# Spectral filter and expert layer: spectral steps of two bins by 256 columns, with the first-factor transform turned over and its output sent through DRAM

## The chip, the cores and the metric

The kernel runs on one core of one Trainium2 chip. The metric is the device time of one execution in microseconds (us). A timed run is made without the profiler; the profile is one more execution, with its own time. TensorE is called PE below, VectorE DVE, ScalarE ACT, GpSimd POOL and SyncE SP, as in the rows of the profile.

## The reference

The input x has 8 sequences of 2496 rows and 256 columns. Along the rows each sequence is filtered in the frequency domain, and each filtered row then goes through one of eight experts.

```python
X = np.fft.rfft(x, axis=1)                      # x: (8, 2496, 256)
Y = X * (filt_r + 1j * filt_i)[None]
y = np.fft.irfft(Y, n=2496, axis=1)             # -> 19968 rows of 256
logits = y @ w_gate                             # 8 experts
expert_idx = argmax(logits); gate = softmax(logits)[expert_idx]
out[row] = gate * (relu(y[row] @ w1[e]) @ w2[e])   # w1: 256x1024, w2: 1024x256
```

## The kernel before

The transform of length 2496 = 39 x 64 is done in two factors, as float32 matrix products. The work is cut into 16 units u: a sequence b and a half h of 128 columns, u = 2b + h.

- `loadx` brings x of one unit into tiles `x` of 39-row groups, three groups on 117 partitions. `forward1` (L263) does the 39-point factor: a piece of x is the stationary operand and the constant `a1` the moving one, so the result stands with the 128 columns on partitions. ACT (and DVE for one of six pieces) copies it, in strides, into the tile `T` (L271).
- A step t is one fifth of a unit: four frequency bins. `spec1` turns `T` back with four TensorE transposes (L311) and ACT copies the result to `z` (L317). `spec2` does the 64-point factor (L326, PSUM tile `px`): four products of 128x128 by 128 columns. `filt_` multiplies by the filter on DVE (L345 to L347), `join` adds the two parts on POOL (L355), `spec3` does the 64-point factor of the inverse (L366, PSUM `pi`), and ACT copies it to `U` (L371). There are 80 steps.
- When a sequence is in `U`, `route1` to `route6` compute the gate and each row's place (L497 and after, PSUM `plw`, `pgl`, `pl`, `pp`), `inv1` turns `U` (L633, PSUM `pg`), `inv2` does the 39-point factor of the inverse (L647, PSUM `py`), and `inv3` scatters the rows, sorted by expert, to the DRAM tile `xs` by indirect DMAs of POOL (L158).
- Beside this, the weights of the experts are loaded (`wf`), brought to a common scale (`w_max` on DVE, L399; `w_hi` on ACT, L465; `w_lo` on DVE, L470), cut into two float16 parts `wh` and stored to DRAM (`wscr`).
- The expert stage reads 161 blocks of 128 sorted rows (`xb`), transposes them by DMA (`xt`), and does the two layers on TensorE (L1038, PSUM `ph`; L1064, PSUM `po`).

The order of the instructions on every engine is written out by hand. Each piece of work is put in a list with a key in steps, `at(key, f, ...)`, the list is sorted by key, and each engine gets its instructions in that order. An engine takes its queue strictly in order; a DMA is issued by the engine in whose queue it stands, and a DMA whose buffer isn't free blocks what stands behind it on that queue. The keys that matter here:

```python
K = {"s2": 1.394, "sr": 1.65, "si": 1.85, "s3": 3.6, "f": 0.063, "fd": 0.75, "w": 6.0, "wp": 4.1}
RT = (0.0, 0.4, 0.45, 0.9, 1.3, 1.7, 2.2, 2.5, 2.9, 3.3)
```

`K["s2"]` is where `spec2` of a step stands behind the step's own key, `K["s3"]` where `spec3` does, and `RT` are the offsets of the ten routing pieces behind the end of a sequence. The PSUM pools are `pF` with 4 banks (for `f`, `pt`, `px`, `pi`, `pg`), `pD` with one, `pY` with two (for `py`) and `pW` with one.

## Time and profile before

| | |
|---|---|
| timed runs | 1387.08, 1389.56, 1389.87 us, median 1389.56 |
| the profiled execution | 1385.97 us, its span 1384.1 us |
| first spectral work, to the first `plw` (sequence 0 done) | 0 to 79.58 us |
| six sequences, from the `plw` of sequence 0 to that of sequence 6 | 79.58 to 428.27 us |
| the rest of the spectral stage, to the first `ph` | 428.27 to 476.54 us |
| the expert stage | 476.54 to 1384.08 us |

`plw` is the first routing product of a sequence and stands right behind its last `spec3`, so the time between two of them is the time of a sequence. Groups in the profile give the busy time, the mean of one instruction and the idle time of the engine ahead of it. Instructions of ACT and PE overlap their neighbours at both ends, so the time that one costs in a full queue is the distance between two starts, shorter than its mean. In the chain of waits the rows are already cut to what each added to the time.

### The profile page before, as it was taken

To read this page: it belongs to the slowest core of one execution; us is meant where nothing else is said; L and a number is where in the kernel's file an instruction comes from. 1 tells how busy PE (TensorE), PEld (TensorE's weight loads), DVE (VectorE), ACT (ScalarE), POOL (GpSimd) and SP (SyncE) were. 2 spreads that over 40 slices of the span, in tenths; PEclk is the share of its full clock that TensorE was granted. 3 is DMA by queue.
4 is the path that set the end of the run, shared out by engine and by line. 5 is a ranking of instruction groups with operands and counts; after the bars stand their busy time and mean duration, and the time that the engine had idled before them with its cause. 6 is when DMAs were issued, how large, how long until landed. Compare 5 with 4: busy or idle time off the path is not lost.

```text
span 1384.1 us, 39837 instructions
## 1 busy us (share of the span) xinstructions
PE 1311.9 (95%) x14855; PEld 1176.2 (85%) x14855; DVE 834.0 (60%) x2391; ACT 853.8 (62%) x1444; POOL 465.2 (34%) x446
## 2 busy tenths in 40 slices
PE   6889999998999799999999989999999999999997
PEld 5778777777777688899999988998999998998997
DVE  1688879888797564455555544555555554555552
ACT  3567667766676546566666655665665665666664
POOL 3627485574745615422111111111111111111111
PEclk9899999999999999999999999999999999999999
DMA  9746565564644533793463396337337336336431
GB/s 181 206 141 201 167 197 178 165 182 149 200 132 126 157 90 94 203 299 91 115 156 82 97 321 205 77 78 190 77 78 193 79 75 191 79 75 162 111 73 43
DMA packets 198278, 197.76 MB, mean 143 GB/s; under 512 B 104008, under 2 KB 177339, under 8 KB 189827
## 3 DMA queue, kind: packets, MB, share of 16 engines
q1 hardware_dynamic: 178142, 151.96, 40.5%
q0 software_dynamic: 19472, 42.51, 10.7%
q8 instruction: 118, 1.93, 0.6%
q10 hardware_dynamic: 468, 0.72, 0.2%
q14 instruction: 78, 0.63, 0.2%
HBM read 344.12 MB, written 61.56 MB: 293 GB/s over the span
## 4 chain that ended last, share of the span: by engine, by line
PE 54%; DMA 7%; DVE 3%; issue 3%; SPq 2%; ACT 1%; POOL 1%; POOLq 0%; DVEq 0%; ACTq 0%
PE ph L1038 26%; PE po L1064 24%; DMA wa<-wscr 3%; DMA wb<-wscr 2%; PE py L647 1%; DMA xt<-xs 1%; SPq L943 1%; SPq L1025 1%; PE pg L633 1%; DMA xs<-yt,dest 1%; PE px L326 1%; PE pi L366 1%; DVE hl L1052 1%; POOL out_dram L158 0%; ACT xs L1017 0%
## 5 line engine op out<-in xcount | busy, mean ns | idle before, releaser
L1038 PE MATMUL ph<-xt,wa 128*128 128x128 f16 x7728 | 462.2, 220 | 12.3 <-DMA wa<-wscr 9.6
L1038 PEld LDWEIGHTS <-wa 128*128 128x128 f16 x7728 | 447.6, 98 | 24.5 <-DMA wa<-wscr 12.7
L1064 PE MATMUL po<-wb,hh 128*128 128x256 f16 x2576 | 431.1, 273 | 4.7 <-ACT ot L1080 2.6
L1052 DVE TENSOR_TENSOR hl<-hs,hh 128x512 f16<-128x512 f32 x322 | 222.8, 692 | 352.6 <-ACT hh L1046 263.8
L158 POOL DMA_INDIRECT out_dram<-ot,t x161 | 157.9, 981 | 672.7 <-DVE xs L1018 571.5
L1064 PE MATMUL po<-wb,hl 128*128 128x256 f16 x1288 | 351.1, 273 | 0.0
L1064 PEld LDWEIGHTS <-hh 128*128 128x128 f16 x2576 | 245.4, 98 | 34.5 <-issue 6.0
L1044 ACT ACTIVATE hs<-ph 128x512 f32<-128x512 f32 x322 | 192.2, 597 | 85.5 <-PE ph L1038 68.4
L158 POOL DMA_INDIRECT xs<-yt,dest x176 | 185.6, 1055 | 120.4 <-issue 62.7
L1017 ACT ACTIVATE xs<-xb,s 128x256 f16<-128x256 f32 x161 | 81.8, 508 | 223.1 <-DVE s L1007 218.4
L1046 ACT CAST hh<-hs 128x512 f16<-128x512 f32 x322 | 198.9, 618 | 10.1
L1064 PEld LDWEIGHTS <-hl 128*128 128x128 f16 x1288 | 126.1, 98 | 14.7
L355 POOL TENSOR_TENSOR p<-tr,ti 128x512 f32<-128x512 f32 x71 | 91.1, 1283 | 93.3 <-DVE ti L347 77.2
L371 ACT COPY U<-pi 128x512 f32<-128x512 f32 (+1 forms) x80 | 87.4, 1092 | 53.5 <-PE pi L366 53.5
L1018 DVE SCALAR_TENSOR_TENSOR xs<-xb,s,xs 128x256 f16<-128x256 f32 x161 | 78.0, 484 | 51.0 <-ACT xs L1017 51.0
L326 PEld LDWEIGHTS px<-z,bm 128*128 128x128 f32 x640 | 80.3, 194 | 20.3 <-issue 10.6
L366 PE MATMUL pi<-cm,p 128*128 128x128 f32 (+1 forms) x640 | 87.7, 281 | 6.2 <-POOL p L355 5.9
L326 PE MATMUL px<-z,bm 128*128 128x128 f32 x640 | 87.9, 281 | 5.6 <-ACT z L317 4.4
L647 PE MATMUL py<-gh,dm 117*117 117x512 f32 x176 | 91.9, 603 | 1.4 <-ACT gh L639 1.4
L263 PE MATMUL f<-a,x 117*128 117x117 f32 (+1 forms) x628 | 87.7, 278 | 5.4 <-ACT U L371 2.1
L366 PEld LDWEIGHTS pi<-cm,p 128*128 128x128 f32 x640 | 80.0, 196 | 9.5 <-POOL p L355 6.3
L263 PEld LDWEIGHTS f<-a,x 117*128 117x128 f32 (+1 forms) x628 | 78.5, 192 | 10.4 <-ACT U L371 3.0
(171 smaller groups left out, 1315.5 us busy)
## 6 DMA issues: line engine op xcount, KB each, us to landing
wb<-wscr SPq DMA_DIRECT2D x133, 1040.0 KB
wa<-wscr SPq DMA_DIRECT2D x133, 1024.0 KB
xb<-xs SPq DMA_DIRECT2D x161, 130.0 KB
wf<-in_moe_w_dram SPq DMA_DIRECT2D x32, 512.0 KB
x<-in_x_dram SPq DMA_DIRECT2D x210, 78.0 KB
wscr<-wh SPq DMA_DIRECT2D x8, 1040.0 KB
wscr<-wh SPq DMA_DIRECT2D x8, 1024.0 KB
xs<-yt,dest POOLq DMA_INDIRECT x176
```

The costliest lines, as they stand in the source:

```text
L158: nc.gpsimd.indirect_dma_start(out=dst, out_offset=bass.IndirectOffsetOnAxis(ap=idx, axis=0), in_=src, in_offset=None, bounds_check=bound, ...
L263: nc.tensor.matmul(ps[:, n : n + m], lhsT=xt.pop((u, g))[:m], rhs=a1[:m, :m], start=True, stop=True,)
L326: nc.tensor.matmul(ps[:, kk], lhsT=bm[:, 4 * it + kk], rhs=z[:, kk], start=True, stop=True,)
L355: e.tensor_tensor(p, tr, ti, op=ALU.add)
L366: nc.tensor.matmul(ps[:, o : o + n], lhsT=p[:, kk], rhs=cm[:, k, :n], start=True, stop=True)
L371: nc.scalar.copy(U[u % NU].rearrange("p n r -> p r n")[:, r0 : r0 + o // 64, :], ps[:, :o].rearrange("p (r n) -> p r n", n=N2),)
L647: nc.tensor.matmul(ps[:GP], lhsT=dm, rhs=gh[:GP], start=True, stop=True)
L1038: nc.tensor.matmul(ps[:, f], lhsT=w[:, p : p + 128], rhs=xt[:, r, c], start=(n == 0), stop=(n == 5))
L1044: nc.scalar.activation(s, ps, AF.Relu, scale=1.0 / B23)
L1046: nc.scalar.copy(hh, s)
L1052: nc.vector.tensor_tensor(hl, s, hh, op=ALU.subtract)
L1064: nc.tensor.matmul(ps, lhsT=h2[q][:, f % 4], rhs=wv[:, r, f], start=(f == 0 and n == 0), stop=(f == 7 and n == 2),)
```

## The change

For sequences 1 to 7 a step is now two frequency bins by all 256 columns, and the 39-point factor is turned over. `forward1` has the constant `ap` (the columns of `a1` in another order) as the stationary operand and two groups of x, 512 columns, as the moving one, so its result stands with the 39 bins on partitions. ACT copies it to a tile `f`, without strides. It has the 64-point index in the free direction and has to get it onto partitions: `spread` stores the tile to a DRAM tile `zd` of its sequence, and `gather` loads it from there into tiles `z` with the 64 values of that index on partitions, in three chunks of 8, 8 and 4 bins. `spec1` and the tile `T` are left out for these sequences. `spec2` has two products of 256 moving columns in place of four of 128. `spec3` has the same four products, and its copy to `U` covers both halves.

Sequence 0 is done in the old way (`head`, `turned`, `spec1`), with `U` buffers that are not in use yet taking the place of `T`. `forward1` of a sequence now stands 11.5 steps ahead of its first step and is spread over 10 steps; its x comes in four chunks of up to 6 KB to a partition, two buffers in turn.

PSUM: `f` has a bank of its own (pool `pE`) and `py` has one bank in place of two. The rest moves small things: `w_max` goes from DVE (a maximum) to ACT (a sum of absolute values), with the scales changed to suit; the copy of `meta` into the rows to be scattered goes from DVE to ACT; the routing offsets and `inv2` move by parts of a step. The expert stage is as it was.

```diff
+    zd = [dram.tile([N2, N1, D], F32, name=f"zd{b}") for b in range(B)]
...
-        pY = early(name="pY", bufs=2, space=PSUM)
+        pY = early(name="pY", bufs=1, space=PSUM)
+        pE = early(name="pE", bufs=1, space=PSUM)
...
+        XC = ((0, 6), (6, 12), (12, 18), (18, 22))
+        ZC = ((0, 8), (8, 16), (16, 20))
...
+        def loadx(b, j):
+            g0, g1 = XC[j]
+            t = xp.tile([GP, 6, D], F32, name=f"x{b}_{j}", tag="x")
+            for l in range(3):
+                n = min(g1, LEN[l]) - g0
+                if n > 0:
+                    nc.sync.dma_start(
+                        t[l * N1 : (l + 1) * N1, :n, :],
+                        split_x(b)[:, 22 * l + g0 : 22 * l + g0 + n, :],
+                    )
+            xt[b, j] = t
...
+        def forward1(b, i):
+            j, q = divmod(i, 2)
+            m = GP if j < 5 else 2 * N1
+            if q == 0:
+                fx[b, j] = xp.tile([GP, 4, D], F32, name=f"f{b}_{j}", tag="f", bufs=2)
+            t, o = xt[b, i // 3], 2 * (i % 3)
+            ps = pE.tile([GP, 2, D], F32, name=f"f1_{b}_{i}", tag="pE")
+            nc.tensor.matmul(
+                ps[:m], lhsT=ap[:m, :m], rhs=t[:m, o : o + 2], start=True, stop=True
+            )
+            nc.scalar.copy(fx[b, j][:m, 2 * q : 2 * q + 2], ps[:m])
+
+        def spread(b, j):
+            f = fx.pop((b, j))
+            g0, g1 = BANKS[j]
+            for l in range(3):
+                n = min(g1, LEN[l]) - g0
+                if n > 0:
+                    nc.sync.dma_start(
+                        zd[b][22 * l + g0 : 22 * l + g0 + n].rearrange("g r d -> r g d"),
+                        f[l * N1 : (l + 1) * N1, :n],
+                    )
...
+        def gather(b, c):
+            k0, k1 = ZC[c]
+            z = tp.tile([128, 8, D], F32, name=f"z{b}_{c}", tag="z")
+            nc.sync.dma_start(z[:N2, : k1 - k0], zd[b][:, k0:k1])
+            k = max(k0, 1)
+            nc.sync.dma_start(z[N2:, k - k0 : k1 - k0], zd[b][:, 19 + k : 19 + k1])
+            zt[b, c] = z
...
         def w_max(e, i, half):
-            nc.vector.tensor_reduce(
-                m[:, half : half + 1],
+            nc.scalar.activation(
+                wh[:, 2048 * half : 2048 * half + 1024].bitcast(BF16),
                 wf[half],
-                axis=AX.X,
-                op=ALU.max,
-                apply_absolute_value=True,
+                AF.Abs,
+                scale=2.0**-10,
+                accum_out=m[:, half : half + 1],
             )
...
-                nc.vector.tensor_copy(yt[:, :, D:], meta[:, 2 * j : 2 * j + 2])
+                nc.scalar.copy(yt[:, :, D:], meta[:, 2 * j : 2 * j + 2])
...
-        RT = (0.0, 0.4, 0.45, 0.9, 1.3, 1.7, 2.2, 2.5, 2.9, 3.3)
+        RT = (0.5, 0.9, 0.95, 1.35, 1.65, 1.95, 2.75, 2.9, 3.2, 3.45)
...
+        for b in range(1, B):
+            z0, d = (10 * b - 11.5, 0.9) if b > 1 else (3.0, 0.55)
+            zs = [z0 + d * i for i in range(11)]
+            for i in range(11):
+                at(zs[i], forward1, b, i)
+                j = i // 2
+                if i % 2 or i == 10:
+                    at(zs[i] + 0.25, spread, b, j)
+            for j in range(4):
+                n = 4 * (b - 1) + j
+                at(xend[n - 2] + 0.02 if n > 1 else 1.0 + 0.4 * j, loadx, b, j)
+                xend[n] = zs[min(3 * j + 2, 10)]
+            for c in range(3):
+                y = (10 * b - 3, 10 * b - 1, 10 * b + 3)[c] if b > 1 or c > 1 else 8 + c
+                at(max(y + K["s2"] + 0.02, zs[10] + 0.7), gather, b, c)
```

Three places show how the queues move. The first is PE in the middle of the spectral stage. Before, about one step of a unit of sequence 5 (`pt` is the transpose of `spec1`, `f` is `forward1`, `px` and `pi` are `spec2` and `spec3`, `pg` and `py` are `inv1` and `inv2`, `pw` belongs to the weights):

```order
L311 MATMUL pt_3165<-ident,T_111 128x128 x4
L263 MATMUL f_10_3_3179<-a_112,x_3_2948 128x117 x4
L326 MATMUL px_3189<-z_3102,bm 128x128 x4
L366 MATMUL pi_3198<-cm,p_3087 128x128 x4
L647 MATMUL py_3_3204<-gh_3_3163,dm 117x512
```

Now, at the change from sequence 1 to sequence 2 (`f_3_2` is `forward1` of sequence 3, `px_1231` the first `spec2` of sequence 2 and the first reader of its gathered chunk `z_0_1070`):

```order
L296 MATMUL f_3_2_1177<-x_0_921,ap 117x512
L382 MATMUL px_1189<-z_2_837,bm 128x256 x2
L425 MATMUL pi_1196<-cm,p_1098 128x128 x4
L707 MATMUL pg_8_1207<-ident,U_130 117x128 x4
L721 MATMUL py_7_1219<-gh_7_1158,dm 117x512
L296 MATMUL f_3_3_1227<-x_1_1017,ap 117x512
L382 MATMUL px_1231<-z_0_1070,bm 128x256 x2
```

The transposes `pt` are gone, `f` is one product in place of four, `px` two in place of four. Between the last `f` of sequence 2 and `px_1231` PE has 4 `pi`, 5 `pg`, 5 `py`, 3 `px`, 4 `f`, one `pw` and one `pv` in its queue. Between the last `f` of sequence 1 and the first reader of its chunk it has 4 `f`, 3 `pi`, 1 `pt`, 2 `px` and one `pw`; for sequence 7 it is 4 `pi`, 5 `pg`, 5 `py`, 3 `px`, one `pw` and one `pv`.

The second place is the DMA queue of SP at the same change. Before, a stretch of the loads of sequence 2 (`x` are loads of x, `wf` and `wscr` belong to the weights):

```order
L248 DMA x_0_1039<-in_x_dram 39x4x128 x3
L482 DMA wscr<-wh_0_986 128x4096
L248 DMA x_1_1088<-in_x_dram 39x4x128 x3
L248 DMA x_2_1141<-in_x_dram 39x4x128 x3
L248 DMA x_3_1187<-in_x_dram 39x4x128 x3
L389 DMA wf_0_1220<-in_moe_w_dram 128x1024 x2
```

Now, around the first chunk of sequence 2 (`zd_61` is its DRAM tile, `f_5` its last tile to be spread, `z_0` and `z_1` its first two chunks, `x_1_1017` a chunk of x of sequence 3):

```order
L556 DMA wscr<-wh_0_821 128x4096
L280 DMA x_1_1017<-in_x_dram 39x1536 x3
L308 DMA zd_61<-f_5_1013 39x2x256 x2
L319 DMA z_0_1070<-zd_61 64x2048
L321 DMA z_0_1070<-zd_61 64x1792
L460 DMA wf_0_1113<-in_moe_w_dram 128x1024 x2
L308 DMA zd_62<-f_0_1076 39x4x256 x3
L280 DMA x_2_1180<-in_x_dram 39x1536 x3
L319 DMA z_1_1192<-zd_61 64x2048
```

The `gather` of `z_0` waits on SP until every `spread` of its sequence has landed, and the loads of the weights, the next `spread` and the next x stand behind it. Per sequence SP has 12 loads of x, 17 stores to `zd` and 6 loads from it, where it had 36 loads of x.

The third place is SP's queue in the first steps. Before:

```order
L248 DMA x_0_271<-in_x_dram 39x4x128 x3
L750 DMA bm<-c_bm_dram 128x512
L285 DMA ff<-in_filt_r_dram 32x1024
L288 DMA ff<-in_filt_r_dram 32x4x256
L285 DMA ff<-in_filt_i_dram 32x1024
L288 DMA ff<-in_filt_i_dram 32x4x256
L248 DMA x_1_300<-in_x_dram 39x4x128 x3
```

Now:

```order
L1223 DMA ap<-c_ap_dram 117x117
L280 DMA x_0_259<-in_x_dram 39x1536 x3
L280 DMA x_1_268<-in_x_dram 39x1536 x3
L824 DMA bm<-c_bm_dram 128x512
L333 DMA ff<-in_filt_r_dram 32x1024
L336 DMA ff<-in_filt_r_dram 32x4x256
L333 DMA ff<-in_filt_i_dram 32x1024
L336 DMA ff<-in_filt_i_dram 32x4x256
```

The second chunk of x of sequence 1, `x_1_268`, takes a buffer that the last piece of sequence 0's second half is read from, so SP waits for that product on PE, and the last part of the constants `bm` and `ff` stands behind it. `ff` is read by POOL (L293, L294 before), which doubles it for `filt_`.

More of the change, by code (lines that the diff above doesn't have):

```diff
@@ L74, in _dft_tables @@
         "a1": np.kron(np.eye(3), a).astype(f32),
+        "ap": np.kron(np.eye(3), a[:, [0, *range(1, N1, 2), *range(2, N1, 2)]]).astype(f32),
         "dm": np.kron(np.eye(3), d).astype(f32),
@@ L120, in tile_fft_moe @@
     NROWS = E * NP + 8 * 128
-    NU = 4
     SEG = []
@@ L310, in spec1, with span @@
                 o = max(0, 2 * (4 * it + kk) - 1) * 64
-                nc.tensor.transpose(
-                    ps[:, kk],
-                    T[u % 2].rearrange("p r n -> p (r n)")[:, o : o + 128],
-                    ident,
-                )
-            z = wp.tile([128, 4, 128], F32, name=f"z{t}", tag="z")
-            nc.scalar.copy(z, ps)
-            stk[t] = z
-        def spec2(t):
-            u, it = divmod(t, 5)
-            z = stk[t]
-            ps = pB.tile([128, 4, 128], F32, name=f"px{t}", tag="pF")
-            for kk in range(4):
+                nc.tensor.transpose(ps[:, kk], Uf[1 + u][:, o : o + 128], ident)
+            z = tp.tile([128, 8, D], F32, name=f"zh{t}", tag="z")
+            nc.scalar.copy(z[:, :4, :128], ps)
+            stk[t] = z
+        def span(t):
+            if t < 10:
+                u, it = divmod(t, 5)
+                return 0, 4 * it, 4, (u,)
+            b, i = divmod(t, 10)
+            return b, 2 * i, 2, (0, 1)
+        def spec2(t):
+            b, k0, nk, hs = span(t)
+            w = 128 * len(hs)
+            if t < 10:
+                z, o = stk[t], 0
+            else:
+                z, o = zt[b, k0 // 8], k0 % 8
+            ps = pB.tile([128, nk, w], F32, name=f"px{t}", tag="pF")
+            for kk in range(nk):
+                m = 128 if k0 + kk else N2
                 nc.tensor.matmul(
                     ps[:, kk],
-                    lhsT=bm[:, 4 * it + kk],
-                    rhs=z[:, kk],
+                    lhsT=bm[:m, k0 + kk],
+                    rhs=z[:m, o + kk, :w],
                     start=True,
@@ L335, in filt_ @@
         def filt_(t):
[L336 to L337 removed]
+            b, k0, nk, hs = span(t)
+            w = 128 * len(hs)
             ps = stk[t]
             fr, fi = (
[L340 removed]
+                ff[:, i, k0 : k0 + nk, 128 * hs[0] : 128 * hs[0] + w] for i in range(2)
             )
[L342 to L343 removed]
+            tr = wp.tile([128, nk, w], F32, name=f"tr{t}", tag="tr")
+            ti = wp.tile([128, nk, w], F32, name=f"ti{t}", tag="ti")
             lo, hi = slice(0, 64), slice(64, 128)
@@ L358, in spec3 @@
         def spec3(t):
-            u, it = divmod(t, 5)
+            b, k0, nk, hs = span(t)
             p = stk.pop(t)
+            n = 64 * (2 * nk - 1 if k0 == 0 else 2 * nk)
             ps = pC.tile([128, 512], F32, name=f"pi{t}", tag="pF")
-            o = 0
-            for kk in range(4):
-                k = 4 * it + kk
-                n = 64 if k == 0 else 128
-                nc.tensor.matmul(
-                    ps[:, o : o + n], lhsT=p[:, kk], rhs=cm[:, k, :n], start=True, stop=True
-                )
-                o += n
-            r0 = max(0, 8 * it - 1)
-            nc.scalar.copy(
-                U[u % NU].rearrange("p n r -> p r n")[:, r0 : r0 + o // 64, :],
-                ps[:, :o].rearrange("p (r n) -> p r n", n=N2),
-            )
+            for h in hs:
+                o = 256 * h if len(hs) > 1 else 0
+                for kk in range(nk):
+                    m = 128 if k0 + kk else 64
+                    q = 128 * h if len(hs) > 1 else 0
+                    nc.tensor.matmul(
+                        ps[:, o : o + m],
+                        lhsT=p[:, kk, q : q + 128],
+                        rhs=cm[:, k0 + kk, :m],
+                        start=True,
+                        stop=True,
+                    )
+                    o += m
+            r0 = max(0, 2 * k0 - 1)
+            if len(hs) > 1:
+                nc.scalar.copy(
+                    U[b % 2].rearrange("p h n r -> p h r n")[:, :, r0 : r0 + n // 64, :],
+                    ps.rearrange("p (h m) -> p h m", h=2)[:, :, :n].rearrange(
+                        "p h (r n) -> p h r n", n=N2
+                    ),
+                )
+            else:
+                nc.scalar.copy(
+                    U[0][:, hs[0]].rearrange("p n r -> p r n")[:, r0 : r0 + n // 64, :],
+                    ps[:, :n].rearrange("p (r n) -> p r n", n=N2),
+                )
         whs = {}
@@ L784, in consts @@
             nc.gpsimd.memset(ones, 1.0)
-            nc.gpsimd.memset(one, 1.0)
             nc.gpsimd.memset(go, 1.0)
@@ L834, in tile_fft_moe @@
             at(t + K["s3"] * rho, spec3, t)
-            if u + 1 < NU_ALL and it == 0:
+            if t == 0:
+                at(0.9, nc.sync.dma_start, ap, cst["ap"])
                 for j in range(6):
-                    at(t + K["f"] + K["fd"] * j, forward1, u + 1, j)
-            if 0 < u and u + 1 < NU_ALL and it == 0:
-                for j in range(6):
-                    n = 6 * (u + 1) + j - 4
-                    v, i = divmod(n, 6)
-                    at(5 * (v - 1) + K["f"] + K["fd"] * i + 0.02, loadx, u + 1, j)
+                    at(t + K["f"] + 0.75 * j, turned, 1, j)
+        for b in range(1, B):
[13 more added lines that the diff above has]
+                at(max(y + K["s2"] + 0.02, zs[10] + 0.7), gather, b, c)
         for i in range(1, 5):
```

110 lines of the change are left out of this document (53 added, 57 removed).

## The prediction

> **What bounds the kernel now.** I read the stages first: the windows of the trace, cut at the first `plw`, at the `plw` of sequence 6 and at the first `ph`. The columns are the stretch, its length, the busy time of PE, PEld, DVE, ACT and POOL with counts, the granted clock, the DMA share and GB/s.
>
> ```profile
> 0.00:79.58 79.58, 61.99 (x432) 55.10 (x432) 38.47 (x62) 39.29 (x50) 35.68 (x33) 0.89 0.82 191
> 79.58:428.27 348.69, 326.28 (x2431) 265.83 (x2431) 292.31 (x572) 243.02 (x359) 210.91 (x192) 1.00 0.55 171
> 428.27:476.54 48.27, 41.33 (x287) 32.00 (x287) 32.63 (x78) 27.77 (x45) 27.46 (x28) 0.96 0.38 115
> 476.54:1384.08 907.54, 882.30 (x11708) 823.24 (x11707) 470.59 (x1683) 543.73 (x991) 191.12 (x195) 0.99 0.49 129
> ```
>
> The change touches the first three rows alone. In the second, the long steady one, PE is busy 326.28 of 348.69 us (94%), DVE 84%, ACT 70%, DMA 55%. Six sequences take 348.69 us, 58.1 us each. The two cuts are these rows of the timeline:
>
> ```profile
> 79.58 0.80 PE L497 MATMUL plw<-U,wg 128*32 128x351 f32 x8
> 428.27 0.80 PE L497 MATMUL plw<-U,wg 128*32 128x351 f32 x8
> ```
>
> Next, the chain of waits in that stage. There its rows follow one another on PE without a gap, so each shows what one piece costs on the path:
>
> ```profile
> 408.75 0.31 PE pv L432 x2
> ...
> 418.63 0.88 PE f L263 x8
> 419.51 0.44 PE pt L311 x4
> 419.95 0.86 PE py L647 x2
> 420.81 0.89 PE px L326 x8
> 421.70 0.44 PE pg L633 x4
> ...
> 423.02 0.90 PE pi L366 x8
> ```
>
> A float32 product is two records, a transpose one. `f`, `px` and `pi` are four products of about 128 columns, `py` one of 512; all cost 0.86 to 0.90 us, so the price goes by columns moved, with 0.03 us more where the stationary operand changes four times. So the spectral stage is bound by PE, and what counts is how many of these pieces the change takes off it.
>
> **The change part by part.**
>
> *PE work.* Per sequence the 39-point factor had 44 products in 11 groups at 0.88 us; now it has 11 products of 512 columns, the form of `py`, at 0.86: 0.2 us less. The ten groups `pt` are gone: 4.4 us. Ten `px` have two products of 256 columns in place of four of 128, 0.86 to 0.89; I take 0.86, since the stationary operand changes half as often: 0.3 us. `pi`, `pg`, `py` stay. That is 4.9 us a sequence, for seven sequences **-34.4 us** (-32.3 if `px` gains nothing).
>
> *Waits of PE.* In the steady stage PE is idle 348.69 - 326.28 = 22.4 us. The group of `plw` shows what a part of it is:
>
> ```profile
> L497 PE MATMUL plw<-U,wg 128*32 128x351 f32 x192 | 17.9, 467 | 5.0 <-ACT U L371 4.6 <-DVE gl L527 0.4
> L271 ACT COPY T<-f 128x468 f32<-128x468 f32 (+1 forms) x61 | 54.1, 887 | 9.9 <-PE f L263 8.8
> L317 ACT COPY z<-pt 128x512 f32<-128x512 f32 x61 | 36.8, 603 | 6.0 <-PE pt L311 5.9
> L639 ACT COPY gh<-pg 117x512 f32<-117x512 f32 x66 | 39.6, 600 | 10.2 <-PE pg L633 10.2
> L465 ACT ACTIVATE wh<-wf,ws 128x1024 f16<-128x1024 f32 x28 | 31.4, 1148 | 4.6 <-DVE ws L443 4.3 <-DVE wx L442 0.3
> L399 DVE TENSOR_REDUCE wm<-wf 128x1 f32<-128x1024 f32 x28 | 33.0, 1211 | 0.2
> L271 DVE COPY T<-f 128x468 f32<-128x468 f32 x12 | 11.7, 978 | 5.9 <-PE f L263 5.9
> L656 DVE COPY yt<-meta 117x8 f32<-117x8 f32 x65 | 23.5, 372 | 0.6
> ```
>
> `plw` waits 5.0 us for the copy to `U` of the last step; the route now begins half a step later, which covers it. DVE loses `wm` 33.0, its share of `T` 11.7 and `yt` 23.5 us: 68.2 of 292.31 us, so waits behind a busy DVE should shrink. ACT loses `T` 54.1 and `z` 36.8; it gains 66 copies like `gh` (39.6), 28 passes of the length of `wh` at 1.15 (32.2), and 65 small copies that no row of ACT shows. These cost more than nothing and less than DVE's 23.5; I take 15, nearer to the 372 ns a piece that this shape has on DVE. That is 4 us less to 15: ACT stays near 239 us, over a stage of some 313 us 76%. So ACT doesn't become the bound. I take 6 us of gain from waits, **-6**; the bound on that side is the whole idle time, -22.4. On the other side `f` has one bank and `py` one for two: the next `f` can't start before ACT has copied the last. Between two `f` PE has at least `pi`, `pg` and `py`, 0.90 + 0.44 + 0.86 = 2.2 us; ACT's copy is 0.60, late by at most two passes of 1.15 in a row, 2.9 in all, so 0.7 us of wait for each such pair. There are 28 / 6 / 2 = 2.3 pairs of `wm` and as many of `wh` a sequence, 3.3 us, +23 over seven as the other bound. Queued behind a waiting `f` are `px` and `pi`, and DVE and POOL wait for those.
>
> *The round trip through DRAM.* Between the last `f` of a sequence and the first reader of its chunk stand: ACT's copy, the issue of a chunk of x that is released at the same moment, the issue and landing of the last `spread`, the issue and landing of the `gather`. None of these transfers is in the trace. The nearest rows: three x loads in SP's queue, scattered rows landing (0.12 MB), blocks `xb` (0.13 MB), weight loads of 1 MB landing, and the DMA rate in two windows, one with the old loads of x (512 bytes a piece), one with pieces of 4 KB and more.
>
> ```profile
> 35.27 1.19 SPq L248 DMA_DIRECT2D x<-in_x_dram  x3
> ...
> 397.35 2.71 DMA xs<-yt,dest
> 462.55 6.48 DMA xs<-yt,dest
> 577.76 3.07 DMA xb<-xs
> 800.83 5.40 DMA wa<-wscr
> 816.96 9.29 DMA wa<-wscr
> ...
> 118.00:120.00 2.00, 2.00 (x18) 1.65 (x17) 1.19 (x5) 1.04 (x2) 1.17 (x2) 1.00 0.99 202
> 130.00:132.00 2.00, 2.00 (x20) 2.00 (x20) 1.76 (x5) 0.96 (x3) 1.78 (x3) 1.00 1.04 427
> ```
>
> Low: 0.60 + 1.2 + 0.8 + 2.71 + 0.8 + 5.40 = 11.5 us. High: with 6.48 and 9.29, 19.2 us. Middle 15.4. The cover is the PE work that the order puts between the two: for sequences 2 to 6 4 `pi`, 5 `pg`, 5 `py`, 3 `px`, 4 `f`, `pw` and `pv`, 3.6 + 2.2 + 4.3 + 2.6 + 3.4 + 0.6 = 16.7 us; for sequence 1, 4 `f`, 3 `pi`, `pt`, 2 `px`, `pw`, 8.7 us; for sequence 7, where no x is loaded and the trip is 10.3 to 18.0 us, 13.3 us. So in the middle sequence 1 waits 6.7, sequence 7 0.9 and the others nothing: **+7.6**. Low 2.9; high 10.5 + 5 x 2.5 + 4.7 = 27.7. The cover of the five is thin: 1.3 us. SP's own wait for the `spread` costs nothing as long as what stands behind it, the next x, is 2.7 steps early.
>
> The Trainium skill ("DMA: Bandwidth & Descriptors", section "Anatomy of one DMA") gives, for DMAs that GpSimd issues, about 2.0 us fixed plus the bytes at 436 GB/s. By that estimate `spread` (0.16 MB) would land in 2.4 and `gather` (0.98 MB) in 4.2 us; the trip would be 10 us, sequence 1 would wait about 1.3 us, and the sum would be 6 us lower. The rows of 1 MB here, 5.40 and 9.29 us, stand above it, so I keep the rows.
>
> *DMA load.* A sequence takes 0.55 x 58.1 = 32 us of all engines. Its x is 2496 KB, 2.56 MB: at 202 GB/s 12.7 us, at 427 GB/s 6.0. Storing `zd` is as much again in pieces of 1 KB, between 6.0 and 12.7; loading it 6.0. So 37 to 44 us of a sequence of some 52: share 0.72 to 0.85. Not the bound, but bursts will meet.
>
> *The start.* PE's queue has `f` of sequence 1 ahead of the first `pi`, where PE waits anyway:
>
> ```profile
> 38.97 2.08 PE L366 MATMUL pi<-cm,p 128*128 128x64 f32 x8 [5.56 <-POOL p L355]
> 40.83 1.19 PE L263 MATMUL f<-a,x 117*128 117x117 f32 x4
> 49.33 1.16 PE L366 MATMUL pi<-cm,p 128*128 128x128 f32 x8 [0.33 <-POOL p L355]
> ...
> 45.16 2.76 POOL L294 TENSOR_SCALAR ff<-ff 64x1024 f32<-64x1024 f32 x1
> 48.01 1.27 POOL L355 TENSOR_TENSOR p<-tr,ti 128x512 f32<-128x512 f32 x1
> ```
>
> So two `f` are free. But the last constants stand behind a load of x that waits for the `f` of the row at 40.83, over at 42. From there: three x issues 1.2, five constant issues 2, landing 3.1 (as `xb`) to 4.7 (1.6 more for 0.7 MB of x at 427 GB/s), POOL's doubling 3.8 (the 2.76 of the row and 1.0 for the copy ahead of it), `p` 1.3. The third `pi` comes at 53.4 to 55 in place of 49.33, 4.1 to 5.7 us late, and PE has done four more `f` by then, 3.4 us. Loss **+2**, bounds 0 and 6.
>
> *The end of the spectral stage.* In the third window PE is busy 41.33 of 48.27 us, and 6.48 us of the rest is the wait for scattered rows (the row at 462.55): DVE's copy of `meta` waits for the buffer, the filter of a step behind it. That wait passes to ACT, and the 4.9 us of PE work taken off sequence 7 are not all won: **+3**, bounds 0 and 4.9.
>
> *Sum:* -34.4 - 6 + 7.6 + 2 + 3 = -27.8. The profiled execution takes 1385.97 us; that gives 1358.2. The median of the runs lies 3.6 us above the profiled execution, so **1362 us**.
>
> **The rivals.**
>
> *The waits go too.* All the idle time of the steady stage, 22.4 us, and the round trip at its low bound: -34.4 - 22.4 + 2.9 = -53.9, with the offset 1336. For it: DVE's relief. Against: PE's idle time is spread over many waits.
>
> *The round trip is late in every sequence.* The high bound: -34.4 + 27.7 + 2 + 4.9, no gain: 1390. For it: the cover is only 1.3 us above the middle. Against: the high bound takes the slowest rows of both transfers together.
>
> *ACT and the single banks.* PE stands behind ACT's long passes: -34.4 + 23 + 7.6 + 2 + 3 = +1, 1391; then the change takes work off PE and PE does not get faster. For it: ACT gains 28 long passes. Against: it is busy 76% only.
>
> *Slower: the DMA rings.* `gather` and `spread` run in SP's ring behind x and a 1 MB store `wscr`. If that store (5.40 us, as a load of its size) lands first every time and the slowest rows hold, the trip is 19.2 + 5.4 = 24.6 us, PE waits 15.9 + 5 x 7.9 + 10 = 65 us: -34.4 + 65 + 2 + 4.9 = +38, 1427. It decides against the change from a wait of 4.9 us a sequence on. For it: the share of up to 0.85. Against: only 0.55 now, with windows of 427 GB/s.
>
> **How the numbers follow.** Forecast, 1350 to 1376: 0.52. The waits go too, below that: 0.17. Late round trip, 1376 to 1392: 0.13. Single banks, same region: 0.06. Slower: 0.12. The range 1335 to 1392 leaves the last out. About 0.2% (2.8 us) is what a measurement of this kernel can tell from no change, so no change is 1387 to 1392. Faster: the first two and half of the next two, 0.78; same: most of the other half, 0.09; slower 0.13.
>
> **What would show it.** The distance of two `plw` at 52 us; `pt` gone but for ten steps; `f` and two `px` products at 0.86 us in the chain. Waits of PE `px` for a DMA of `z` of 5 to 7 us in sequence 1, about none later. `f` or `py` waiting for ACT above 1 us a sequence would speak for the banks; a DMA share above 0.9 with `z` waits in every sequence for the rings. A forecast that is wrong will most likely be wrong in the round trip or in the waits, since the PE work is counted from rows.

## The result, and the profile after

The changed kernel takes 1406.51 us (median of four runs, 1401.62 to 1411.71) against 1388.47 us before: ratio 1.013, 95% interval 1.0091 to 1.0170. It is **slower** by 18 us; the forecast was 1362 us, 28 us faster. The profiled execution took 1401.62 us, the fastest of the four, and its span is 1399.8 us.

The windows of the trace after, cut at the same places as those of before: the first `plw`, the `plw` of sequence 6, the first `ph` (columns as in the prediction).

```profile
0.00:103.68 103.68, 74.02 (x370) 53.45 (x370) 35.89 (x60) 44.55 (x64) 35.53 (x32) 0.85 0.84 203
103.68:438.33 334.65, 297.16 (x1544) 191.13 (x1543) 223.91 (x466) 230.71 (x420) 211.66 (x191) 0.98 0.88 266
438.33:486.29 47.96, 36.44 (x215) 25.66 (x216) 31.15 (x66) 23.93 (x49) 29.47 (x31) 0.99 0.42 131
486.29:1399.80 913.51, 880.77 (x11708) 823.48 (x11708) 469.32 (x1667) 545.33 (x1002) 189.50 (x193) 0.99 0.50 128
```

Against before the stages are **+24.1, -14.0, -0.3 and +6.0 us**, together the 15.7 us between the two spans. In the second row PE has 29.1 us less work (326.28 to 297.16) but the stage is only 14.0 us shorter: PE's idle time went up, from 22.4 to 37.5 us. DVE lost 68.4 us and ACT 12.3.

**The start.** PE's timeline after, at the places that the prediction costed:

```profile
38.14 2.02 PE L296 MATMUL f<-x,ap 117*117 117x512 f32 x2 [6.93 <-DMA x<-in_x_dram]
...
43.70 1.05 PE L425 MATMUL pi<-cm,p 128*128 128x64 f32 x8
...
53.00 1.09 PE L351 MATMUL pc<-ident,bm 128*128 128x128 f32 x4 [5.35 <-DMA bm<-c_bm_dram]
53.88 1.91 PE L425 MATMUL pi<-cm,p 128*128 128x128 f32 x8
55.58 1.91 PE L296 MATMUL f<-x,ap 117*117 117x512 f32 x2
...
60.11 1.06 PE L425 MATMUL pi<-cm,p 128*128 128x128 f32 x8
...
79.66 2.03 PE L296 MATMUL f<-x,ap 117*117 117x512 f32 x2 [2.02 <-DMA x<-in_x_dram]
81.48 1.91 PE L425 MATMUL pi<-cm,p 128*128 128x64 f32 x8
```

The first `f` of sequence 1 stands ahead of the first `pi` and waits 6.93 us for its x. The first `pi` comes at 43.70 (38.97 before), the third at 60.11 (49.33 before, 53.4 to 55 forecast). SP's queue and the DMA share at that time:

```profile
26.54 19.93 SPq L280 DMA_DIRECT2D x<-in_x_dram  x6
46.52 0.35 SPq L824 DMA_DIRECT2D bm<-c_bm_dram  x1
```

```profile
0.00:40.00 40.00, 23.68 (x134) 17.62 (x135) 5.85 (x9) 12.75 (x17) 15.15 (x15) 0.89 0.85 165
40.00:50.00 10.00, 7.65 (x49) 6.31 (x47) 5.10 (x7) 4.13 (x7) 4.68 (x3) 0.93 0.34 82
50.00:103.68 53.68, 42.70 (x189) 29.52 (x189) 24.95 (x44) 27.68 (x40) 15.70 (x15) 0.81 0.92 253
```

SP stood 19.93 us at six loads of x, since the second chunk had no free buffer, with the last constants behind it. From 40 to 50 us the DMA engines were busy to 0.34 only (0.57 before); afterwards to 0.92.

**The steady stage.** Its chain of waits shows the pieces at about the price that was forecast, 0.86 us for `f` and 0.87 for a pair of `px`:

```profile
266.29 0.86 PE f L296 x2
...
267.59 0.87 PE px L382 x4
```

New are stops like this one, in the timeline of all engines (start and length in us, engine, line, and in brackets the idle time before and what ended it):

```profile
228.04 1.06 ACT L474 ACTIVATE wh<-wf 128x1024 bf16<-128x1024 f32 x1
228.22 0.68 DVE L403 TENSOR_TENSOR ti<-px,ff 64x512 f32<-64x512 f32 x1
...
229.08 0.58 ACT L299 COPY f<-f 117x512 f32<-117x512 f32 x1
229.55 1.07 ACT L474 ACTIVATE wh<-wf 128x1024 bf16<-128x1024 f32 x1
...
230.74 0.16 DVE L482 SCALAR_TENSOR_TENSOR wm<-wm 128x1 f32<-128x1 f32 x1 [1.84 <-ACT wh L474]
...
231.01 0.33 DVE L656 TENSOR_REDUCE rsm<-rex 117x22 f32<-117x176 f32 x1
...
231.15 0.38 PE L497 MATMUL pw<-ident,wm 128*1 128x128 f32 x2 [1.43 <-DVE wm L485]
```

ACT now finds the maxima of a weight tile, two passes with an `f` copy between them; DVE joins the two results (L482) and waits for the second, with the routing (L656) and the next filter behind it; PE's `pw` waits for DVE, with a `pi` behind it. In the stage DVE waits 42.9 us in 12 such places.

### The profile page after: what moved, and what is told of

Read it like the earlier page. It is cut to its first block, busy times and chain, and to the rows that moved or that the text cites. A ratio compares the mean times of both kernels' runs of the same rounds, so it can differ in the third digit from the quotient of the medians.

```text
span 1399.8 us, 37657 instructions
## 1 busy us (share of the span) xinstructions
PE 1288.4 (92%) x13833; PEld 1093.7 (78%) x13833; DVE 760.3 (54%) x2257; ACT 844.5 (60%) x1533; POOL 466.2 (33%) x445
## 4 chain that ended last, share of the span: by engine, by line
PE 68%; DMA 11%; DVE 8%; ACT 5%; issue 5%; SPq 2%; POOL 1%; POOLq 0%; DVEq 0%; ACTq 0%
PE ph L1123 27%; PE po L1149 26%; DMA wa<-wscr 3%; PE py L721 3%; PE pi L425 3%; PE px L382 3%; PE f L296 2%; DMA x<-in_x_dram 2%; PE pg L707 1%; PE plw L571 1%; ACT wh L474 1%; DMA bm<-c_bm_dram 1%; DMA zd<-f 1%; DVE wh L544 1%; ACT wh L539 1%
## 5 line engine op out<-in xcount | busy, mean ns | idle before, releaser
L425 PEld LDWEIGHTS pi<-cm,p 128*128 128x128 f32 x640 | 85.5, 200 | 28.0 <-issue 19.7
L435 ACT COPY U<-pi 128x512 f32<-128x512 f32 (+1 forms) x70 | 76.0, 1086 | 35.9 <-PE pi L425 35.9
L296 PE MATMUL f<-x,ap 117*117 117x512 f32 (+1 forms) x154 | 85.1, 635 | 12.6 <-DMA x<-in_x_dram 9.5
L1165 ACT ACTIVATE ot<-po,g 128x256 f32<-128x256 f32 x161 | 73.7, 458 | 26.2 <-PE po L1149 12.2
L382 PE MATMUL px<-z,bm 128*128 128x256 f32 (+1 forms) x280 | 78.6, 401 | 11.4 <-DVE ti L403 7.4
L401 DVE TENSOR_TENSOR tr<-px,ff 128x512 f32<-128x512 f32 x80 | 54.9, 686 | 62.3 <-PE px L382 39.7
```

The source lines that it names most:

```text
L296: nc.tensor.matmul(ps[:m], lhsT=ap[:m, :m], rhs=t[:m, o : o + 2], start=True, stop=True)
L382: nc.tensor.matmul(ps[:, kk], lhsT=bm[:m, k0 + kk], rhs=z[:m, o + kk, :w], start=True, stop=True,)
L425: nc.tensor.matmul(ps[:, o : o + m], lhsT=p[:, kk, q : q + 128], rhs=cm[:, k0 + kk, :m], start=True, stop=True,)
```

## The experiments

The chips of these runs are slower than that of the result: the kernel before takes 1414 to 1417 us there. So each run is held against the kernel before on its own chip, and stages against those of `c0_after` (the changed kernel) and `c1_before`. Stages of unchanged work differ by up to 3 us from chip to chip in the steady stage and by up to 8 us behind it (920.3 us in `c2_b1`, 912.5 in `b1_place`, the same kernel). A window is that of one profiled execution, and that can lie away from the median of the runs: 6.4 us above it in `e4_fromx`, 6.0 in `e7_nomax2`, 7.6 in `c2_b1`, 9.8 in `b3_wmax`, 3.8 below it in `e9_place`. So the ratio, taken from the timed runs, decides what an edit is worth in the whole, and the windows say where. A letter stands for a chip; the times are those of the windows, in us.

| run | chip | ratio to before (95%) | first `plw` | six sequences | sequence 7 | the rest |
|---|---|---|---|---|---|---|
| `c1_before` | D | | 81.9 | 350.6 | 66.2 | 919.7 |
| `c0_after` | C | 1.0074 (1.0061 to 1.0087) | 105.1 | 337.2 | 63.6 | 917.7 |
| `e1_consts` | B | 1.0074 (1.0052 to 1.0095) | 107.3 | 335.3 | 67.1 | 916.5 |
| `e2_start` | B | 1.0024 (1.0001 to 1.0047) | 103.1 | 334.7 | 64.2 | 917.2 |
| `e3_wmax` | B | 1.0087 (1.0064 to 1.0110) | 105.9 | 340.4 | 66.4 | 917.2 |
| `e4_fromx` | B | 1.0030 (1.0012 to 1.0047) | 106.9 | 334.6 | 64.7 | 919.5 |
| `e5_nomax` | C | 1.0140 (1.0125 to 1.0154) | 104.4 | 353.6 | 64.2 | 911.0 |
| `e6_nostore` | C | 0.9955 (0.9941 to 0.9970) | 100.2 | 324.4 | 67.7 | 913.3 |
| `e7_nomax2` | D | 1.0007 (0.9988 to 1.0025) | 104.9 | 333.0 | 64.7 | 919.5 |
| `e8_bplace` | D | 0.9963 (0.9949 to 0.9976) | 81.1 | 346.0 | 63.1 | 920.1 |
| `e9_place` | E | 0.9898 (0.9866 to 0.9930) | 100.4 | 316.3 | 63.0 | 914.4 |
| `e10_b1nostore` | E | 0.9821 (0.9791 to 0.9851) | 94.9 | 315.2 | 62.3 | 914.8 |
| `b1_place` | C | **0.9892** (0.9862 to 0.9923) | 101.5 | 317.5 | 63.1 | 912.5 |
| `c2_b1` (the same kernel) | E | **0.9864** (0.9838 to 0.9889) | 100.4 | 315.4 | 67.6 | 920.3 |
| `b2_late` | D | 0.9904 (0.9882 to 0.9925) | 98.1 | 324.5 | 65.0 | 917.4 |
| `b3_wmax` | E | 1.0205 (1.0178 to 1.0233) | 99.2 | 368.3 | 66.2 | 921.3 |

The theories at first: A, the start loses by SP's order; B, the maxima on ACT cost the steady stage; C, the way of `f` through DRAM does, by its length (C1) or by its load (C2).

**The start in two edits.** `e1_consts`:

```diff
-        at(1.9, loadk, bm, "bm", 4, 5)
-        at(1.91, loadf, 4, 5)
+        at(0.92, loadk, bm, "bm", 4, 5)
+        at(0.93, loadf, 4, 5)
```

> One edit: the last constants (bm and ff of steps 16 to 19) are issued ahead of the first two pieces of x for sequence 1, not behind them. Theory A (the start, 24.1 us later at the first plw than before, is lost in SP's order): the waits for bm (5.35 us) and for ff (POOL's 9.30 us) go, and with them the halved clock behind them, but the x piece lands some 4 us later and f of sequence 1, which stands ahead of the first pi, waits about 4 us more than its 6.93: the first plw moves from 103.7 to 98 to 102, the whole by -2 to -6 us, near 1402. Theory B (DVE held up by the maxima on ACT) and theory C (the round trip and the DMA load in the steady stage): nothing after the start changes, and the first plw stays within 2 us of 103.7.

`e2_start` has that too, and

```diff
-            z0, d = (10 * b - 11.5, 0.9) if b > 1 else (3.0, 0.55)
+            z0, d = (10 * b - 11.5, 0.9) if b > 1 else (4.65, 0.40)
```

> The edit of e1_consts, and f of sequence 1 begins at key 4.65 in steps of 0.40 in place of 3.0 and 0.55, so that two f no longer stand ahead of the first pi; the last f of sequence 1 stays at about the same key (8.65 for 8.5). Theory A: both holes of the start (6.93 us for x, 5.35 for bm) and the slow clock behind them go; the first plw comes at 88 to 94 us in place of 103.7, and the whole falls by 10 to 15 us, to about 1393. Rival: PE's holes in the start are only moved to the later waits for x and for ACT's copies, since the 17 f and their stores have to be done there anyway and the DMA share is 0.84: the first plw comes at 99 or later and the whole gains less than 4 us.

The constants alone won nothing (ratio 1.0074, first `plw` at 107.3, a miss). With `f` moved as well the holes at 38 and 53 us are gone, yet the first `plw` comes at 103.1, as the rival said: PE stops later instead (PE's timeline in `e2_start`).

```profile
45.90 1.02 PE L296 MATMUL f<-x,ap 117*117 117x512 f32 x2
...
60.86 1.73 PE L296 MATMUL f<-x,ap 117*117 117x512 f32 x2 [2.02 <-DMA x<-in_x_dram]
...
70.39 1.12 PE L296 MATMUL f<-x,ap 117*117 117x512 f32 x2 [2.33 <-ACT f L299]
...
75.05 2.03 PE L296 MATMUL f<-x,ap 117*117 117x512 f32 x2 [1.86 <-DMA x<-in_x_dram]
...
92.42 2.37 PE L382 MATMUL px<-z,bm 64*128 64x256 f32 x4 [4.53 <-DMA z<-zd]
```

So the two holes were real, but they held only a small part of the 24 us: the ratio falls from 1.0074 (`e1_consts`, same chip) to 1.0024, some 7 us, which is more than the rival's 4, and the first `plw` comes 4.2 us earlier than in `e1_consts`. What is left stands behind the transfers of sequence 1.

**The maxima back on DVE**, `e3_wmax`:

```diff
-            nc.scalar.activation(
-                wh[:, 2048 * half : 2048 * half + 1024].bitcast(BF16),
-                wf[half], AF.Abs, scale=2.0**-10,
-                accum_out=m[:, half : half + 1],
-            )
+            nc.vector.tensor_reduce(
+                m[:, half : half + 1], wf[half],
+                axis=AX.X, op=ALU.max, apply_absolute_value=True,
+            )
```

> One edit: the maxima of the weights go back from ACT (a pass with Abs that also accumulates) to DVE's maximum, as before the change, with the constants of the scale as before. Theory B (in the steady stage DVE stands behind ACT's pass, 42.9 us in 12 waits of the instruction that joins the two maxima, and the filter behind it): the stage from the first plw to that of sequence 6 goes from 334.7 to 315 to 325 us, DVE's wait at that instruction goes to about nothing, and the whole falls by 10 to 20 us. Theory C (round trip and DMA load): DVE has slack anyway, the wait is one that costs nothing, and the stage stays within 3 us of 334.7, or gets longer, since DVE gets 33 us of work more. The start is not touched by either: within 2 us of 103.7.

340.4 us, not 315 to 325: B falls in this form, and with it 33 us of work are back on DVE for only 3 us more of stage than in `c0_after`.

**z from x**, `e4_fromx`, with the stores still made; and **no stores either**, `e6_nostore` (`if n > 0:` in `spread` never true):

```diff
-            nc.sync.dma_start(z[:N2, : k1 - k0], zd[b][:, k0:k1])
+            xk = x[b].rearrange("(p k) d -> p k d", k=N1)
+            nc.sync.dma_start(z[:N2, : k1 - k0], xk[:, k0:k1])
```

> One edit: the pieces z are loaded from x itself (same sizes and addresses of the same form), not from the place in DRAM where f was stored; f is still computed and stored. So no z waits for a store, while the bytes moved stay the same; what is left out is that the first factor of the transform reaches the rest in sequences 1 to 7. Theory C1 (the chain f, store, load is late): waits of px for z go, the steady stage goes from 334.7 to 322 or less, and the start is 2 to 4 us shorter. Theory C2 (not the chain, but the load on the DMA engines, share 0.88) and theory B: the stage stays within 3 us of 334.7, with the share at 0.88.

> z is loaded from x, as in e4_fromx, and the stores of f are left out as well, so that 2.56 MB a sequence less are moved and the first factor of the transform doesn't reach the rest in sequences 1 to 7. The share of the DMA engines in the steady stage should fall from 0.88 to 0.65 to 0.75. Theory C2 (the load on the DMA engines delays x, z, the weights and the scattered rows, and through them PE): the steady stage goes from 334.7 to 322 or less, and the first plw comes 6 to 12 us earlier. Theory D: the start gets shorter in the same way, but the steady stage stays within 4 us of 334.7.

Without the dependency the steady stage takes 334.6 us in the profiled execution, within what chips differ by, and the start is no shorter (106.9). So C1 falls for the stage, where 322 or less was expected. The whole is another matter: 1.0030 against 1.0074 of `e1_consts` on the same chip, 6 to 7 us. The profiled execution lies 6.4 us above the median, so the windows don't show where these 6 to 7 us are, and the price of the round trip stays open up to that size. Without the stores the steady stage takes 324.4 us, between the two forecasts, and the first `plw` comes 4.9 us earlier. C2 seems to hold, 12.8 us of 337.2 (10.2 against `e4_fromx`, on another chip); a later run changes the reading.

**The anchor**, `c0_after`, the changed kernel itself, on the chip of `e5`, `e6` and `b1`:

> The changed kernel itself, so that the edits are held against it on one chip. All theories: 1.3% slower than before (1.009 to 1.017), the first plw near 104 to 110 us, some 55 to 57 us from one plw to the next.

It is 0.74% slower than before here, less than on the chip of the result and below the expected 0.9%, and `c1_before` shows where, on a chip on which the kernel before takes about as long:

> The kernel before itself, for its stages on this chip. Theory E (the end of the spectral stage is no faster after the change): from the plw of sequence 6 to that of sequence 7 it takes 53 to 56 us here too, against 63.6 in the changed kernel. Rival: the 57 to 67 us of the changed kernel belong to the chip, and the kernel before takes over 60 us here. First plw at 79 to 83, steady stage 348 to 356, the rest 903 to 918 us.

Start +23.2, six sequences -13.4, sequence 7 -2.6, the rest -2.0. The first two repeat the result; the 6.0 us that the expert stage took longer there do not come again. Sequence 7 takes 66.2 us in the kernel before too (one execution): theory E falls.

**No maxima at all**, twice. `e5_nomax` puts a constant in place of the two passes and has POOL write it, `e7_nomax2` has DVE write it:

```diff
-            nc.scalar.activation(... AF.Abs, scale=2.0**-10, accum_out=m[:, half : half + 1])
+            nc.gpsimd.memset(m[:, half : half + 1], 2.0**-14)     # e5_nomax
+            nc.vector.memset(m[:, half : half + 1], 2.0**-14)     # e7_nomax2
```

> The two passes of ACT over each weight tile that find its maximum are left out, and the constant 2 to the -14 stands in their place (written by POOL; the real maxima have the same exponent), so that nobody pays for the maxima. 28 passes of 1.06 us and 28 reads of 0.20 leave the steady stage, 35 us of ACT, and with them DVE's wait for them (42.9 us). Theory D (with PE's work gone, the first half of a sequence, in which the routing and the weights run, is bound by ACT and DVE in turn): the steady stage goes from 334.7 to 315 to 324 us. Theory C2 (DMA load): it stays within 3 us of 334.7. Theory B in its strong form, that the maxima only had to be put back on DVE, has fallen with e3_wmax, where the stage took 340.4 us.

> As e5_nomax, but the constant is written by DVE itself, so that no instruction of DVE waits for POOL any more (in e5_nomax it waited 36.9 us, because POOL's write stood behind its scatters, and PE's pw waited 22 us for DVE). Theory D: with the maxima gone and no new wait the steady stage goes from 337.2 to 317 to 328 us. Rival F (what counts is where in the sequence the weights' steps stand, since PE's pw and pv stand in order before the spectral pieces and wait for DVE, not how much ACT does): the stage stays above 331.

`e5_nomax` does less work than the changed kernel and takes 16.4 us longer in the steady stage (9.6 us in the whole, by the medians). The waits of that stage (engine, line, waits for; us in all, times, longest) say why:

```profile
DVE wm L476 <- POOL wm L474: 36.9, 7, 8.2
...
PE pw L491 <- DVE wm L479: 19.2, 7, 4.2
```

POOL's write stands behind its scatters, DVE behind POOL, PE behind DVE. With the constant on DVE the stage takes 333.0 us: 35 us of ACT's passes (26 us of its busy time, since they overlap) and DVE's wait for them are gone, for 4 us in the stage. By the ratios, 1.0007 against 1.0074, the whole gains some 9 us. So the forecast of D for this run, 317 to 328 us, is missed, and the amount of ACT's work is at most the smaller part. Rival F is left: what counts is where in the sequence the weights' chain (ACT, DVE, `pw`, DVE, `pv`, DVE, ACT, DVE) meets the routing's.

**The weights' work placed by hand**, `b1_place`, on top of `e2_start`:

```diff
+        WZ = sorted([10 * m + y for m in range(7) for y in (6.3, 9.4)] + [42.8, 52.8])
         for q in range(2 * E):
             e, i = divmod(q, 2)
-            z = K["w"] + K["wp"] * q
+            z = WZ[q]
```

> The two edits of e2_start, and the work on a weight tile is placed by hand in the second half of a sequence (keys 6.3 and 9.4 of each ten, two more at 42.8 and 52.8) and no longer at every 4.1 keys, so that it mostly doesn't meet the routing. Theory D: in the sequences with two tiles the distance of two plw goes from 54 to 58 down to 51 to 53 us, the steady stage to 312 to 325 us, and the kernel is faster than before by 0.2 to 0.8%. Theory C2: the stage stays within 3 us of 334.7, and the kernel is as in e2_start, 0.2% slower than before.

> b1_place again, to hold the next three against it on one chip. All theories: 0.987 to 0.992 of before, first plw at 100 to 103 us, steady stage 316 to 322.

The steady stage falls to 317.5 and 315.4 us, and the kernel is 1.1 and 1.4% **faster than before**. The steady windows of `c1_before`, `c0_after` and `b1_place`:

```profile
81.88:432.46 350.58, 328.22 (x2432) 266.85 (x2431) 292.36 (x572) 242.81 (x359) 211.60 (x192) 1.00 0.54 170
```

```profile
105.10:442.31 337.21, 298.27 (x1543) 191.52 (x1542) 225.19 (x468) 230.21 (x419) 212.03 (x192) 0.97 0.88 265
```

```profile
101.53:419.07 317.54, 289.39 (x1544) 187.48 (x1543) 236.08 (x466) 229.45 (x420) 216.32 (x191) 1.00 0.91 280
```

The same PE and ACT work, at a higher DMA share (0.91). Of the 19.7 us, 10.8 are PE's idle time (38.9 to 28.2) and 8.9 are busy time, for the granted clock is back at 1.00. DVE's wait for ACT's passes goes from 36.0 us in `c0_after` to 14.8. The stage is now within 2 to 5 us of the 313 us that the prediction had for it, on other chips. PE's longest waits are another list now, `c0_after` first, then `c2_b1`:

```profile
PE px L382 <- DVE ti L403: 7.3, 3, 3.6
PE pw L497 <- DVE wm L485: 5.0, 5, 1.4
...
PE plw L571 <- ACT yt L730: 4.1, 2, 2.9
```

```profile
PE pw L497 <- DVE wm L485: 7.5, 6, 1.6
...
PE plw L571 <- ACT yt L730: 1.5, 2, 1.2
```

The wait of `px` for the filter, 7.3 us in three stops, is gone; that of `pw` for the weights' chain is longer.

**Is it the placement's own gain?** The same edit in the kernel before, `e8_bplace`, and alone in the changed kernel, `e9_place`:

> The kernel before, with only the placement of the work on the weights of b1_place (no other edit). Theory D: there PE is busy 94% of the steady stage, so the placement can win no more than a part of 22 us of idle time, and its waits were spread: the stage gains 0 to 6 us, the kernel 0 to 0.4%. Rival G (the placement is a gain of its own that the change has nothing to do with): it gains 15 to 20 us here as well, ratio 0.985 to 0.99.

> The placement of b1_place alone, without its two edits of the start. If the start edits win little by themselves, since the DMA engines bind the rest of the start, the first plw comes at 103 to 106 us, the steady stage takes 316 to 322 as in b1_place, and the ratio is 0.990 to 0.996. If the start edits carry a part of the steady gain (e2_start had none), the steady stage takes over 325.

In the kernel before it wins 4.6 us in the steady stage and 0.37%; in the changed kernel it alone gives 316.3 us, some 20 less than without, and takes the ratio from 1.0074 to 0.9898. That fits a PE that, busy 94%, covered the chain before. The first `plw` comes at 100.4 as in `c2_b1`. So on top of the placement the two edits of the start win nothing that these runs can tell (0.9898 and 0.9864, with intervals that overlap). One rival is open: the change also moved the routing by up to half a step (`RT`), and no run puts that back alone, so how much of the meeting comes from these keys and how much from PE's shorter cover is not separated.

**What is left.** `e10_b1nostore` (`b1_place`, `z` from x and no stores), `b2_late` (no weight tile in the first sequence) and `b3_wmax` (`b1_place` with the maxima on DVE):

```diff
-        WZ = sorted([10 * m + y for m in range(7) for y in (6.3, 9.4)] + [42.8, 52.8])
+        WZ = sorted([10 * m + y for m in range(1, 7) for y in (6.3, 9.4)] + [32.8, 42.8, 52.8, 62.8])   # b2_late
```

> b1_place with z loaded from x and no store of f (the first factor of the transform doesn't reach the rest in sequences 1 to 7). Theory H (what is left of the loss in the start is the round trip's own load and order on the DMA engines): the first plw comes at 88 to 94 us in place of 101.5. Rival (it is the work of PE, ACT and DVE that is done ahead, with the slow clock behind each stop): 97 to 101. The steady stage: if the load of the stores costs what it did without the placement (12.8 us), 303 to 308; if the placement has already taken it away, 314 to 318.

> b1_place with no weight tile in the first sequence (4 MB of loads and stores less before the first plw); sequences 2 to 5 take three instead. If the rest of the start is bound by the DMA engines (share 0.82 and more from 50 us on, x and z late by 3.9 and 3.6 us), the first plw goes from 101.5 to 94 to 98 us; the steady stage, at a share of 0.91, gets longer by 3 to 8 us, and the kernel is between 0.985 and 0.992 of before. If the start is bound by something else, the first plw stays at 100 or more and the kernel gets slower than b1_place.

> b1_place with the maxima on DVE, as before the change. If DVE, at 236 us of 317 busy, has room now that the weights stand outside the routing, the wait for ACT's pass (14.8 us) goes and the stage falls to 310 to 315, ratio 0.984 to 0.988. If it is DVE's order that counts, the filter stands behind the maxima and the stage goes up by 3 to 10 us.

The steady windows of `c2_b1` and `e10_b1nostore`:

```profile
100.44:415.89 315.45, 290.28 (x1544) 188.71 (x1543) 237.62 (x466) 230.27 (x420) 216.69 (x191) 0.99 0.91 283
```

```profile
94.94:410.14 315.20, 292.82 (x1543) 191.51 (x1543) 232.14 (x465) 230.39 (x420) 215.92 (x192) 0.97 0.79 234
```

Without the stores the DMA share falls from 0.91 to 0.79 and the steady stage takes 315.2 us, as with them (315.4): their load costs this stage nothing that the runs can tell once the weights stand elsewhere. The 12.8 us of `e6_nostore` were a delay that mattered only to an order already tight. In the start the stores are worth 5.5 us (100.4 to 94.9), between H and its rival; the two weight tiles 2 to 3 us, from chip to chip (98.1 in `b2_late`, which gives back more in the steady stage: 324.5). Against the 81.9 us of the kernel before 13.1 us remain without the stores. The windows of the start, of `c1_before` and of `e10_b1nostore`:

```profile
0.00:81.88 81.88, 62.66 (x432) 55.92 (x432) 38.46 (x62) 39.32 (x50) 35.68 (x33) 0.90 0.83 185
```

```profile
0.00:94.94 94.94, 70.68 (x369) 51.29 (x369) 35.69 (x60) 44.66 (x64) 35.50 (x32) 0.89 0.83 192
```

8.0 us of them are PE's work, 5.0 its idle time; no run took this work out of the start, so its share is read from the windows and not tested. The groups of `f` in the start (after, then before; busy time, mean in ns, idle time ahead) say what that work is. Of two records a product, there are 17 products of 512 columns now, the 11 of sequence 1 and six of sequence 2. Before there were 44 products of a quarter of that size, six of sequence 0 and 38 of the 44 of sequence 1.

```profile
L296 PE MATMUL f<-x,ap 117*117 117x512 f32 (+1 forms) x34 | 21.9, 731 | 12.4 <-DMA x<-in_x_dram 9.5 <-ACT f L299 2.9
```

```profile
L263 PE MATMUL f<-a,x 117*128 117x117 f32 (+1 forms) x88 | 13.0, 285 | 1.9 <-PE pt L311 1.0 <-ACT z L317 0.7 <-DVE ti L347 0.2
```

`b3_wmax` takes 368.3 us in the steady stage, 53 more than `c2_b1` (49 in the whole, by the medians), for 33 us of DVE work at places where the filter stands behind it; 3 to 10 were expected. So with this order the move of the maxima to ACT was right, and what DVE has to spare on average (237.6 of 315.4 us busy in `c2_b1`) says nothing of what it has at one place.

## Why the prediction was wrong

The sum was -27.8 us against the span and what lies around it; +15.7 came. Step by step:

- *PE work, -34.4: right in kind.* 29.1 us less in the steady stage, 29.4 forecast for six sequences. But 5.2 us of these are six `f` of 0.86 us that the start had done ahead (60 of 66 stand in this stage), and a part of the busy time ran at a lower clock (0.98). At a clock of 1.00 (`b1_place` against `c1_before`) it is 38.8 less 5.2 us, 5.6 a sequence for 4.9.
- *Waits of PE, -6: the step that failed first.* PE's idle time rose by 15.1 us, 21 us from the forecast. The premises held: DVE lost 68.4 us (68.2 forecast), ACT stands at 230.7 us, 69% (239 and 76%). The inference "so waits behind a busy DVE should shrink" did not hold. `plw` alone still waits 3.7 us for ACT (1.2 for the copy to `U`, 2.5 for the copies of `meta`), where 5.0 were to go. In place of the gain: the chains of the routing and the weights, which PE had covered with its own 94%, came to the surface where they meet. The placement takes some 20 us off the stage in the changed kernel (`e9_place`) and 4.6 in the one before (`e8_bplace`). The wait that the change added to the weights' chain, DVE for ACT's passes (42.9 us), is the smaller part: without the passes the stage is 4 us shorter and the whole some 9 (`e7_nomax2`). The 22.4 us of idle time before were no store to draw on, and my bound on the other side looked only at the banks.
- *The single banks, the +23 bound: did not come.* In the steady stage `f` waits 0.2 us in all for ACT, `py` 1.7.
- *The round trip, +7.6: too much.* `px` waited 1.6 us for `z` in the start (6.7 forecast for sequence 1) and 0.9 after it. That PE's waits for `z` are hidden in the other sequences was right; what the dependency costs in other ways, up to 7 us, is open (`e4_fromx`). The transfers themselves were often slow, as the rows of 1 MB had it: the chain of waits has 7.35 us for a `z`, and 2.65 and 11.23 for a store of 0.16 MB.

```profile
64.40 2.65 DMA zd<-f
...
100.18 11.23 DMA zd<-f
...
196.39 7.35 DMA z<-zd
```

  The estimate in the prediction from the Trainium skill ("DMA: Bandwidth & Descriptors", section "Anatomy of one DMA"), for DMAs that GpSimd issues, was 4.2 us for a `z` and 2.4 us for a store. On SP's queue here one store comes near it, and the other two rows stand far above it.
- *DMA load, no term.* The share was 0.88, just above the forecast's 0.85, and "not the bound" was half right: the load of the stores cost up to 12.8 us of the steady stage by way of a tight order, and nothing there without it.
- *The start, +2 (bounds 0 and 6): the largest miss, +24.1.* Two errors. "So two `f` are free" took PE's idle time before the first `pi` as room, without asking when their x lands: PE stood 6.93 us for it, and the first `pi` behind it came 4.7 us later than before. This was the smaller one; with it mended the first `plw` came some 4 us earlier (`e2_start`). The larger one: I closed the account at the third `pi`, forecast at 55 at the latest (it came at 60.11). What followed wasn't costed: 17 `f`, 2.56 MB stored and two of its three chunks loaded again before the first `plw`, and PE stops of up to 2 us, at a share of 0.92. The stores are worth 5.5 us of this; of the 13.1 us that are left without them 8.0 are PE's work.
- *The end of the spectral stage, +3 on -4.9: about right*, -0.3 by the cut at the first `ph`. The +6.0 us of the expert stage did not come again.

The rival on the slower side had the sign and not the cause: `z` waits in every sequence did not appear. Of "what would show it", the distance of two `plw` was 55.8 us for 52; with the weights' work moved it is 52.6 to 52.9.

## What to carry to other kernels

When work is taken off the engine that binds, list the chains through the other engines that it had covered, and cost them at the places where they meet, not by the share of busy time. An engine's room on average is no room at a given place in its queue: moving the same maxima, 33 us of work, from ACT to DVE cost 3 us of the steady stage in one order of the weights' work (`e3_wmax`) and 53 in another (`b3_wmax`). A look-ahead is paid where it begins: count all that the first sequence has to do ahead, and when its data land, before calling idle time free.
